# Moving an attention kernel's input loads into one software DMA queue, with the last rows grouped per head pair

## Chip, cores, metric

The kernel runs on one core of one Trainium2 chip. The metric is device time in microseconds (us), the median of several executions. Single-core executions of one kernel mostly agree within about 1% here. A span in a profile is that of one profiled execution, about 2 us shorter than its timed value.

## The reference, cut to what matters

```python
# q, k, v: (8 batches, 8 heads, 576 rows, 64) float32; w_phi: (64, 128)
def phi(x):
    proj = einsum('bhsd,df->bhsf', x, w_phi)
    proj = proj - max(abs(proj), -1)
    return concatenate([exp(proj), exp(-proj)], -1)
# linear attention: num = phi(q) @ (phi(k)^T v), den = phi(q) @ sum(phi(k)); x = num/den
# then, per batch on (576, 512):
X = rfft(x, axis=1)[:64 modes];  Y = X (complex) times w_r + i w_i per mode  # 64 x 512 x 512, twice
u = x + irfft(Y);  out = u + relu(u @ w_ch)                                   # w_ch: 512 x 512
```

The two weight tensors are 134 MB of float32, q, k and v together 28 MB. Everything else is small.

## The kernel before

The attention stage handles 16 units: 4 head pairs `g` times 4 batch pairs `bp`. Loads are issued by two engines. POOL issues loads on the software queue, here with a cast from float32 to bfloat16 on the way; SP (the sync engine) issues loads on the hardware queue, here without a cast. Rows 512 to 575 of each (batch, head), the "tails", come separately:

```python
def load(t, rest, src, g, bp, eng):
    for i in range(2):
        hs = src[2 * bp + i, 2 * g:2 * g + 2]
        sp.dma_start(rest[64 * i:64 * i + 64],                       # tail: 128 runs of 256 B, hardware queue
                     hs[:, 512:576, :].rearrange("h p d -> p h d"))
        eng.dma_start(                                               # main: 128 partitions x 2 x 1 KB
            t[:, 8 * i:8 * i + 8, :].rearrange("p (h c) d -> p h (c d)", h=2),
            hs[:, 0:512, :].rearrange("h (p c) d -> p h (c d)", c=4))
# k, q: main by POOL with cast, tail as float32 and cast by VectorE (cast_k, cast_q)
# v:    main and tail by SP, float32
```

Weights come as 64 tiles of 1 MB (bfloat16, 2 MB read) by POOL, in eight rotating buffers (five early tiles sit elsewhere). Each is used by one `mix`; a mix frees its buffer and the next tile is issued. After the attention loop, PE runs the remaining 22 mixes and 36 `channels` steps (x @ w_ch), which need `wchb`, the bfloat16 copy of w_ch:

```python
    wchb = const.tile([128, 4, 512], BF16, name="wchb")
...
        if n == 6:                                   # in the attention loop
            pool.dma_start(wchb, moe_w_ch.rearrange("(dc p) e -> p dc e", p=128))
...
pm_cm.__exit__(...); pin_cm.__exit__(...)            # attention memory ends
pb = pb_cm.__enter__()
while mixq:
    mix(...); next_w(1)                              # next_w issues one weight tile
    for _ in range(2):
        if todo: channels(*todo.pop(0))
```

Each engine works off a fixed list. In the built program PE's order at this point is: mix 42, mix 43, four channels, mix 44, mix 45, four channels, and so on (counted from zero).

The softmax here doesn't subtract the row's maximum and nothing guards it: scores larger than these inputs give would overflow.

## Time and profile before

| | before |
|---|---|
| time, median of 3 | 481.94 us (481.29 to 482.75) |
| span of the profiled execution | 481.0 us |
| mix 43 starts | 325.0 us |
| first channels step | 326.1 us |
| last mix (tile 63) starts | 432.9 us |
| output stage starts | 438.7 us |

From the page of the kernel before: span, DMA busy in 40 slices (9 is 90% or more), the two load queues, the chain that ended last, and some DMA issues (size, median us from issue to landing). PE multiplies matrices, DVE is VectorE, ACT is ScalarE.

```profile
span 481.0 us, 8083 instructions
...
DMA  8999999999999999999999999999999999990676
...
q0 software_dynamic: 84496, 76.03, 97.2%
q1 hardware_dynamic: 26784, 23.14, 18.4%
...
DMA 9%; PE 9%; ACT 0%; DVE 0%; issue 0%; POOL 0%; ACTq 0%; POOLq 0%
...
wt<-in_moe_w_i_dram POOLq DMA_DIRECT2D x30, 1024.0 KB, 27.1
...
vn<-in_v_dram SPq DMA_DIRECT2D x32, 256.0 KB, 8.0
...
kb<-in_k_dram POOLq DMA_DIRECT2D x32, 128.0 KB, 20.9
```

The packets of the software queue took 97% of the 16 engines' span. A weight tile waits 27 us to land, while v on the hardware queue takes 8 us.

From the table by windows of the same kernel: length and busy us per engine, then PE's granted clock, DMA share and GB/s written. A share above 1 means packets overlap on an engine.

```profile
12.00:330.00 318.00, 220.34 (x2472) 153.66 (x2469) 236.10 (x429) 201.74 (x345) 83.13 (x105) 0.82 1.25 210
330.00:430.00 100.00, 67.02 (x478) 30.74 (x477) 20.64 (x43) 27.98 (x49) 10.49 (x12) 0.95 1.23 212
```

The DMA share stays at the same level through both stages, so I take DMA to pace the kernel up to 430 us; the chain that ended last agrees, with 43.9 us of DMA for the last weight tile.

From PE's timeline (start, duration, engine, line, operation, count, and in brackets the idle time before it and what ended it):

```profile
319.99 0.69 PE L37 MATMUL one<-wt,XT_69 128*32 128x512 bf16 x8 [2.78 <-DMA wt<-in_moe_w_r_dram]
...
325.04 1.09 PE L37 MATMUL one<-wt,XT_69 128*32 128x512 bf16 x8 [4.03 <-DMA wt<-in_moe_w_i_dram]
326.06 1.89 PE L469 MATMUL one<-wchb,xT 128*128 128x512 bf16 x4
...
432.87 1.09 PE L37 MATMUL one<-wt,XT_70 128*32 128x512 bf16 x8 [5.06 <-DMA wt<-in_moe_w_i_dram]
...
438.70 0.58 PE L607 MATMUL pt<-xs,ident_b 128*128 128x512 bf16 x1 [0.72 <-ACT zst L37]
```

These are mixes 42 and 43, the first channels step (wchb long there), the last mix and the start of the output stage. Between 325 and 433 us the mixes wait now and then for their tile, but those waits are only about 15 us out of the 112 us from 326.1 to 438.7 us: PE has little slack.

### The profile page before, as it was taken

How to read it: one execution, taken by the hardware profiler on the slowest of the kernel's cores; microseconds unless marked ns; L12 is line 12 of the kernel's file. 1: busy time of each engine (PE TensorE's matmuls, PEld its weight loads, DVE VectorE, ACT ScalarE, POOL GpSimd, SP SyncE). 2: the span in 40 equal slices, each digit the busy share in tenths (PEclk: the TensorE clock that was granted, in tenths of full speed). 3: DMA queues.
4: the chain of work that ended last, by engine and by line, in shares of the span. 5: the costliest groups of instructions: out<-in, count | busy, mean ns of one | idle time of the engine just before them, and what ended most of it. 6: DMA issues, size and time to landing. Idle time of an engine off the chain costs nothing. (4 is left out here: it accounts for less than half of the span.)

```text
span 481.0 us, 8083 instructions
## 1 busy us (share of the span) xinstructions
PE 329.9 (69%) x3133; PEld 202.0 (42%) x3133; DVE 288.8 (60%) x524; ACT 256.4 (53%) x435; POOL 103.9 (22%) x139
## 2 busy tenths in 40 slices
PE   2563786778877876876597546827667676738994
PEld 1351554555555544654365334613233332312441
DVE  5777579778679779778869747622222121100874
ACT  3771867867867965865675737401223232301763
POOL 8332222123312331322033121221111110000000
PEclk9956879777889988878977959788899999965998
DMA  8999999999999999999999999999999999990676
GB/s 137 212 213 210 210 209 210 214 213 191 216 210 211 213 215 207 214 216 205 215 218 203 220 204 207 207 207 208 207 207 218 214 214 214 215 178 22 241 296 251
DMA packets 111318, 99.68 MB, mean 207 GB/s; under 512 B 16944, under 2 KB 109744, under 8 KB 110256
## 3 DMA queue, kind: packets, MB, share of 16 engines
q0 software_dynamic: 84496, 76.03, 97.2%
q1 hardware_dynamic: 26784, 23.14, 18.4%
q8 instruction: 24, 0.39, 0.3%
q14 instruction: 14, 0.11, 0.1%
HBM read 163.64 MB, written 9.44 MB: 360 GB/s over the span
## 5 line engine op out<-in xcount | busy, mean ns | idle before, releaser
L37 ACT ACTIVATE AB<-two 128x1024 bf16<-128x1024 f32 x64 | 62.0, 1021 | 44.3 <-DVE mk L37 43.9
L37 ACT ACTIVATE AQ<-two 128x1024 bf16<-128x1024 f32 x64 | 62.6, 1042 | 17.4 <-PE two L37 17.3
L471 ACT CAST xw<-one 128x512 bf16<-128x512 f32 x36 | 21.1, 585 | 68.8 <-PE one L469 57.6
L466 DVE COPY xT<-one 128x512 bf16<-128x512 bf16 x36 | 15.3, 424 | 63.9 <-PE one L464 63.9
L37 POOL DMA_DIRECT2D wt<-in_moe_w_r_dram x29 | 25.6, 882 | 111.5 <-PE one L37 66.3
L469 PE MATMUL one<-wchb,xT 128*128 128x512 bf16 x144 | 39.0, 395 | 14.0 <-DVE xT L466 14.0
L37 PE MATMUL one<-va,AB 128*128 128x65 bf16 x512 | 31.8, 227 | 20.6 <-DVE va L37 20.6
L37 DVE TENSOR_TENSOR va<-vn,ee 128x1152 bf16<-128x1152 f32 x32 | 41.9, 1352 | 0.0
L37 DVE TENSOR_REDUCE mk<-two 128x8 f32<-128x1024 f32 x32 | 39.0, 1218 | 4.0 <-PE two L37 4.0
L37 PE MATMUL one<-kvz,AQ 128*128 128x65 bf16 x512 | 30.2, 205 | 15.5 <-ACT kvz L37 10.7
L37 DVE TENSOR_REDUCE mq<-two 128x8 f32<-128x1024 f32 x32 | 37.6, 1215 | 1.1 <-PE two L37 1.1
L37 PEld LDWEIGHTS <-AB 128*128 128x128 bf16 x512 | 26.8, 120 | 26.7 <-DVE va L37 13.1
L37 POOL DMA_DIRECT2D wt<-in_moe_w_i_dram x30 | 26.4, 880 | 49.8 <-PE one L37 19.3
L37 PEld LDWEIGHTS <-AQ 128*128 128x128 bf16 x512 | 25.8, 106 | 26.3 <-issue 23.0
L37 POOL DMA_DIRECT2D qb<-in_q_dram x32 | 22.9, 719 | 57.3 <-PE one L37 16.3
L37 POOL DMA_DIRECT2D kb<-in_k_dram x32 | 22.9, 717 | 52.7 <-DMA wt<-in_moe_w_i_dram 17.5
L37 PE MATMUL one<-ident_b,kb 128*128 128x128 bf16 x144 | 15.3, 254 | 25.0 <-DMA kb<-in_k_dram 16.1
L620 DVE TENSOR_TENSOR of<-pt,rl 128x512 f32<-128x512 f32 x32 | 21.7, 690 | 15.1 <-ACT rl L618 14.8
L37 PE MATMUL one<-wt,XT_70 128*32 128x512 bf16 x256 | 20.6, 418 | 14.6 <-DMA wt<-in_moe_w_i_dram 11.9
L37 DVE TENSOR_TENSOR nd<-one,nd 128x390 f32<-128x390 f32 x48 | 27.1, 565 | 5.7 <-PE two L37 0.5
L618 ACT ACTIVATE rl<-pt 128x512 f32<-128x512 f32 x36 | 21.4, 597 | 15.3 <-PE pt L609 12.4
L37 PE MATMUL one<-CF,xs 128*128 128x256 bf16 x160 | 26.7, 327 | 2.3 <-DVE xs L37 2.3
(125 smaller groups left out, 620.5 us busy)
## 6 DMA issues: line engine op xcount, KB each, us to landing
wt<-in_moe_w_i_dram POOLq DMA_DIRECT2D x30, 1024.0 KB, 27.1
wt<-in_moe_w_r_dram POOLq DMA_DIRECT2D x29, 1024.0 KB, 26.5
vn<-in_v_dram SPq DMA_DIRECT2D x32, 256.0 KB, 8.0
out_dram<-of SPq DMA_DIRECT2D x8, 1024.0 KB, 3.9
kb<-in_k_dram POOLq DMA_DIRECT2D x32, 128.0 KB, 20.9
qb<-in_q_dram POOLq DMA_DIRECT2D x32, 128.0 KB, 17.1
kf<-in_k_dram SPq DMA_DIRECT2D x32, 32.0 KB, 6.1
vn<-in_v_dram SPq DMA_DIRECT2D x32, 32.0 KB, 6.8
```

Of the source, the lines that this page charges most:

```text
L37: ins = f(*args, **kwargs)
L466: nc.vector.tensor_copy(xT, pt)
L469: nc.tensor.matmul(pf, lhsT=xT[:, g, :], rhs=wchb[:, g, :], start=(g == 0), stop=(g == 3))
L471: nc.scalar.copy(xw[:, bp, n, :], pf)
L618: nc.scalar.activation(rl, ps[1], ACT.Relu)
L620: nc.vector.tensor_tensor(out=o, in0=ps[0], in1=rl, op=ALU.add)
```

## The change

The intent is to drop the hardware queue's many small loads and VectorE's casts: everything goes through the software queue, v too but without a cast, and the tails of a head pair are fetched once for all batches (4 loads per tensor and head pair, in place of 2 per unit and tensor). The grouped tails need more memory, so wchb no longer fits beside the attention stage and moves behind it.

```diff
-    def load(t, rest, src, g, bp, eng):
+    def load(t, src, g, bp, eng):                       # main part only, as before
...
+    def load_rests(name, src, g, eng):
+        t = pin.tile([128, NP, 2, D_], F32 if name == "v" else BF16, name=name + "r")
+        for i in range(2):
+            for h in range(2):
+                eng.dma_start(
+                    t[64 * i:64 * i + 64, :, h, :],
+                    src[i::2, 2 * g + h, 512:576, :].rearrange("b p d -> p b d"))
+        rests[name, g] = t
...                                                      # cast_k, cast_q gone; va multiply regrouped
-                unit(n + 3).load_v()                     # by SP
+                unit(n + 3).load_v(pool)
+        if n >= 0 and n % 4 == 0 and n // 4 + 1 < NG:    # behind load_k
+            load_rests("k", k, n // 4 + 1, pool)
+        if n >= 0 and n % 4 == 1 and n // 4 + 1 < NG:    # behind load_v
+            load_rests("q", q, n // 4 + 1, pool)
+            load_rests("v", v, n // 4 + 1, pool)
...
-    wchb = const.tile([128, 4, 512], BF16, name="wchb")
-        if n == 6:
-            pool.dma_start(wchb, ...)
+    wchb = pb.tile([128, 4, DMODEL], BF16, name="wchb", bufs=1)      # behind the attention loop
+    nc.gpsimd.dma_start(wchb, ...)
```

The v of the first two units and the v tails of the first head pair still come by SP.

More of the change, by code (lines that the diff above doesn't have):

```diff
@@ L87 @@
     pm = pm_cm.__enter__()
-    def load(t, rest, src, g, bp, eng):
+    def load(t, src, g, bp, eng):
         for i in range(2):
-            hs = src[2 * bp + i, 2 * g:2 * g + 2]
-            sp.dma_start(
-                rest[64 * i:64 * i + 64],
-                hs[:, 512:576, :].rearrange("h p d -> p h d"),
-            )
             eng.dma_start(
                 t[:, 8 * i:8 * i + 8, :].rearrange("p (h c) d -> p h (c d)", h=2),
-                hs[:, 0:512, :].rearrange("h (p c) d -> p h (c d)", c=4),
-            )
+                src[2 * bp + i, 2 * g:2 * g + 2, 0:512, :].rearrange(
+                    "h (p c) d -> p h (c d)", c=4),
+            )
+    rests = {}
+    def load_rests(name, src, g, eng):
[6 more added lines that the diff above has]
+        rests[name, g] = t
     class Unit:
@@ L107, in load_k, with load_v, turn @@
         def load_k(self):
-            self.kb = pin.tile([128, 18, D_], BF16, name="kb")
-            self.kf = pin.tile([128, 2, D_], F32, name="kf")
-            load(self.kb, self.kf, k, self.g, self.bp, pool)
-        def cast_k(self):
-            dve.tensor_copy(self.kb[:, 16:18, :], self.kf)
-        def load_q(self):
-            self.qb = pin.tile([128, 18, D_], BF16, name="qb")
-            self.qf = pin.tile([128, 2, D_], F32, name="qf")
-            load(self.qb, self.qf, q, self.g, self.bp, pool)
-        def cast_q(self):
-            dve.tensor_copy(self.qb[:, 16:18, :], self.qf)
-        def load_v(self):
-            self.vn = pin.tile([128, 18, D_], F32, name="vn")
-            load(self.vn, self.vn[:, 16:18, :], v, self.g, self.bp, sp)
-        def turn(self, src, name):
+            self.kb = pin.tile([128, 16, D_], BF16, name="kb")
+            load(self.kb, k, self.g, self.bp, pool)
+        def load_q(self):
+            self.qb = pin.tile([128, 16, D_], BF16, name="qb")
+            load(self.qb, q, self.g, self.bp, pool)
+        def load_v(self, eng):
+            self.vn = pin.tile([128, 16, D_], F32, name="vn")
+            load(self.vn, v, self.g, self.bp, eng)
+        def turn(self, src, rest, name):
             dst = pm.tile([128, 9, 128], BF16, name=name, tag="xT", bufs=3)
             flat = src.rearrange("p n d -> p (n d)")
+            rest = rest[:, self.bp].rearrange("p h d -> p (h d)")
             for lo, hi in ((0, 4), (4, 9)):
@@ L133, in turn @@
                 for j in range(lo, hi):
-                    pe.transpose(ptr[:, j - lo, :], flat[:, j * 128:(j + 1) * 128], ident_b)
+                    x = flat[:, j * 128:(j + 1) * 128] if j < 8 else rest
+                    pe.transpose(ptr[:, j - lo, :], x, ident_b)
                 act.copy(dst[:, lo:hi, :], ptr)
@@ L138, in turn_k @@
         def turn_k(self):
-            self.kT = self.turn(self.kb, "kT")
+            self.kT = self.turn(self.kb, rests["k", self.g], "kT")
             self.mk = pm.tile([128, 2, 18], F32, name="mk")
         def turn_q(self):
-            self.qT = self.turn(self.qb, "qT")
+            self.qT = self.turn(self.qb, rests["q", self.g], "qT")
             self.mq = pm.tile([128, 18], F32, name="mq")
@@ L191, in weigh_v2 @@
             dve.tensor_copy(self.va[:, :, :, 64], ee)
-            for ab in range(2):
+            for n0, n1, x in ((0, 16, self.vn), (16, 18, rests["v", self.g][:, self.bp])):
+                shape = [128, 2, n1 - n0, 64]
                 dve.tensor_tensor(
-                    out=self.va[:, ab, :, 0:64], in0=self.vn,
-                    in1=ee[:, ab, :].unsqueeze(2).to_broadcast([128, 18, 64]), op=ALU.mult,
+                    out=self.va[:, :, n0:n1, 0:64], in0=x.unsqueeze(1).to_broadcast(shape),
+                    in1=ee[:, :, n0:n1].unsqueeze(3).to_broadcast(shape), op=ALU.mult,
                 )
@@ L320 @@
     units[0].load_k()
-    units[0].load_v()
+    load_rests("k", k, 0, pool)
+    units[0].load_v(sp)
+    load_rests("v", v, 0, sp)
     units[0].load_q()
+    load_rests("q", q, 0, pool)
     w2blk = const.tile([128, 256], BF16, name="w2blk")
@@ L495 @@
     units[1].load_k()
-    units[1].load_v()
+    units[1].load_v(sp)
     next_w(1)
@@ L499 @@
     next_w(1)
-    units[0].cast_k()
     units[0].turn_k()
@@ L523 @@
                 mixq += [(P.g, mg) for mg in range(2 * NO)]
-        if K:
-            K.cast_q()
         if Q:
             Q.num(0)
-        if R:
-            R.cast_k()
         if K:
@@ L569 @@
         some(X - 4)
-        if n == 6:
-            pool.dma_start(wchb, moe_w_ch.rearrange("(dc p) e -> p dc e", p=128))
     for e in (pe, dve, act, pool, sp):
@@ L578 @@
     pb = pb_cm.__enter__()
+    wchb = pb.tile([128, 4, DMODEL], BF16, name="wchb", bufs=1)
+    nc.gpsimd.dma_start(wchb, moe_w_ch.rearrange("(dc p) e -> p dc e", p=128))
     xw = pb.tile([128, NP, 9, DMODEL], BF16, name="xw", bufs=1)
```

## The prediction

> **What bounds the kernel now.** The table by windows gives a DMA share of 1.23 to 1.26 from 12 to 410 us (packets overlap). Most loads stand in the software queue: a 1 MB weight tile takes 26.5 us from issue to landing (DMA issues), the last ones 43.9 us. Fitting packet counts to elapsed time, I estimate per engine and packet: weights (1 KB) 79.8 ns, q/k (512 B) 43, v (1 KB, hardware queue) 53, tails (256 B) 26. So a weight tile costs 5.1 us, and 64 of them 327 us. The chain of waits ends with 43.9 us of DMA for the last weight tile (to 432.8 us), then 48 us of final mix and output.
>
> **What the change does.**
> 1. Tails: 12,288 packets before and after, but 48 issues instead of 96, now mostly on the software queue, q and k cast to 128 B. Cost before 768 x 26 ns = 20 us per engine. The Trainium skill (DMA: Bandwidth & Descriptors, Specifications) says that under 512 B the engine does read-modify-write; the trace shows only 256 B at 26 ns. I expect 15 to 28 ns: -8 to +2 us.
> 2. v: 512 packets per engine, 53 ns to 43-50 ns: -1 to -5 us.
> 3. DVE loses 32 casts of 0.22 us; the va multiply keeps its element count. Little is critical.
> 4. POOL issues some 106 more small loads at 0.71 us (75 us). The program lets only eight software-queue loads be outstanding (each waits for the eighth before it), so runs of 12 to 22 small loads leave little queued: I expect short DMA gaps where the tails go, 2 to 8 us in all.
>    Sum of 1 to 4: the stream to weight tile 49 gains about 2 us (-6 to +8).
> 5. wchb moves. It was loaded at 156 us, needed at 326 us. Now it takes over memory of the attention stage and stands in the POOL order behind weight tile 49. The queue being first in first out (43.9 us for eight tiles agrees), wchb lands just after tile 49, which the timeline shows arriving at 355.4 us. In PE's program order its first user (channels) follows mix 43 (done at 326.1 us), and PE cannot pass it. So PE stands still until about 354 us, then has nearly all of the second stage to do: 326.1 to 438.7 us before, about 15 us of it waits for weight tiles, so 97.5 us of PE chain. It was just hidden under DMA (10.1 us of PE chain, 10.2 us of DMA per two tiles), so PE can't catch up.
>
> **Sum.** 355.4 - 2 + 97.5 + 42.3 (output stage, 438.7 to 481) = 493 us, plus 1 us for time over span, plus about 2 us [...]: **496 us, range 488 to 507**. Chances: faster 0.02, within 2% 0.23, slower 0.75.
>
> **What would show it.** PE (channels) waits some 28 us once for wchb; POOL issues the last weight tile after 400 us; the chain that ended last is PE/DVE/ACT from about 354 us on rather than DMA. kb/qb land sooner, v later (8 us to about 15-20 us).
>
> **What would make it wrong.** Tails or v much cheaper in the software queue, or attention freed by 10 us or more (then within 2%); wchb landing earlier than tile 49; a late v stalling DVE, or DMA gaps over 10 us (then above 500).

## The result, and the profile after

The changed kernel took 500.52 us (median of 4, 500.29 to 503.86) against 481.62 us (median of 4). The ratio is 1.0408, 95% interval 1.0358 to 1.0458. Ratios here and below are the mean time of one kernel's fast runs over that of the other's of the same rounds, so not quite the ratio of the medians quoted.

From the page of the changed kernel, the same lines:

```profile
span 498.5 us, 7899 instructions
...
DMA  9999999999999999999999999999999999961576
...
q0 software_dynamic: 95824, 85.21, 103.3%
q1 hardware_dynamic: 6432, 12.91, 7.5%
...
PE 8%; ACT 1%; DVE 1%; DMA 1%; issue 0%; ACTq 0%
...
wt<-in_moe_w_i_dram POOLq DMA_DIRECT2D x30, 1024.0 KB, 19.2
...
vn<-in_v_dram POOLq DMA_DIRECT2D x28, 256.0 KB, 14.1
kb<-in_k_dram POOLq DMA_DIRECT2D x32, 128.0 KB, 14.2
```

The chain that ended last was half DMA and half PE (9% of the span each); now it is nearly all PE (8%, DMA 1%). A weight tile now lands after 19 us, which fits with less standing ahead of it in the queue. From the table by windows:

```profile
12.00:330.00 318.00, 207.72 (x2434) 146.49 (x2449) 231.46 (x396) 201.65 (x343) 129.25 (x173) 0.83 1.20 200
330.00:430.00 100.00, 51.47 (x361) 23.55 (x367) 16.32 (x34) 20.72 (x36) 12.28 (x14) 0.80 1.19 202
```

The DMA share fell from 1.25 to 1.20 and from 1.23 to 1.19. The first figure looks small; over 318 us it is about 13 us of lost DMA time. From PE's timeline:

```profile
326.31 1.10 PE L37 MATMUL one<-wt,XT 128*32 128x512 bf16 x8 [2.75 <-DMA wt<-in_moe_w_r_dram]
...
331.33 1.09 PE L37 MATMUL one<-wt,XT 128*32 128x512 bf16 x8 [3.38 <-DMA wt<-in_moe_w_i_dram]
364.40 0.58 PE L474 MATMUL one<-wchb,xT 128*128 128x512 bf16 x1 [31.98 <-DMA wchb<-in_moe_w_ch_dram]
...
458.06 0.38 PE L612 MATMUL pt<-xs,ident_b 128*128 128x512 bf16 x1 [0.72 <-ACT zst L37]
```

Mix 43 comes 6.3 us later than before (331.33 against 325.04). Then PE stands still for 32.0 us until wchb lands. Weight tiles had been landing about 5.07 us apart (the mixes that waited for tiles 43 and 49 started at 325.04 and 355.44 us before). Six tiles and wchb, half a tile, make 6.5 x 5.07 = 33.0 us; from 331.33 to 364.40 is 33.1 us. So wchb came exactly in its turn. From 364.40 to 458.06 us PE works off what it had hidden under DMA before.

To see where the DMA time went, I added up the packets' times in each microsecond, divided by 16 engines, and summed what is missing to 1.24, the undisturbed level; the sum over 12 to 330 us, divided by 1.24, is called the shortfall below. It is 3.7 us before and 19.0 us after. (Where the microseconds are cut moves these sums by up to 0.6 us, so smaller differences of the shortfall mean nothing.) The largest holes after are at 62 to 64, 92 to 94, 164 to 166 and 243 to 248 us. POOL's timeline shows the second of them:

```profile
78.50 1.30 POOL L37 DMA_DIRECT2D qr<-in_q_dram  x2
84.21 0.62 POOL L37 DMA_DIRECT2D qr<-in_q_dram  x1 [4.41 <-DMA wt<-in_moe_w_i_dram]
89.25 0.61 POOL L37 DMA_DIRECT2D qr<-in_q_dram  x1 [4.43 <-DMA xs<-in_moe_w_r_dram]
89.89 2.09 POOL L37 DMA_DIRECT2D vr<-in_v_dram  x3
92.18 0.62 POOL L37 DMA_DIRECT2D vr<-in_v_dram  x1 [0.20 <-DMA qr<-in_q_dram]
92.79 1.45 POOL L37 DMA_DIRECT2D qb<-in_q_dram  x2
94.21 0.93 POOL L37 DMA_DIRECT2D xs<-in_moe_w_i_dram  x1
```

The q tails (`qr`) wait for weight tiles to land although they need nothing from them. The built program explains it. Every load on the software queue takes one of eight semaphores in turn and waits until the load that used it last has landed. POOL's order in the built changed kernel, numbered in its own list, with those waits (DMASW is the semaphore):

```
57 vn<-in_v_dram 128x2x256 [waits DMASW1_49,DVE_49]
58 vn<-in_v_dram 128x2x256 [waits DMASW2_49]
59 qr<-in_q_dram 64x4x64 [waits DMASW3_49]
60 qr<-in_q_dram 64x4x64 [waits DMASW4_49]
61 qr<-in_q_dram 64x4x64 [waits DMASW5_49]
62 qr<-in_q_dram 64x4x64 [waits DMASW6_49]
63 vr<-in_v_dram 64x4x64 [waits DMASW7_49]
...
69 xs<-in_moe_w_i_dram 128x8x512 [waits DMASW5_49]     (a weight tile)
```

So the tails hold up POOL until the weight tiles ahead have landed. When the last of them has (89.2 us), only small loads are outstanding, and POOL needs some 5 us to issue seven more small loads before the next weight tile follows at 94.2 us. DMA runs dry meanwhile. All in all POOL waited 22.8 + 17.7 us at q tails for weight tiles. From its list of waits (who waited for what, us in total, times, longest):

```profile
POOL qr L37 <- DMA wt<-in_moe_w_i_dram: 22.8, 5, 5.0
POOL qr L37 <- DMA wt<-in_moe_w_r_dram: 17.7, 4, 5.0
```

POOL waits for weight tiles before the change too (17.5 us at kb loads, for example). What is new is how much small work follows: counted in the built programs, behind the start, the longest stretch of small loads between two weight tiles grows from 8 to 20.

The packets of v got cheaper, and the others hardly changed (packet records of the two traces; sizes are those written):

| packet | before | after |
|---|---|---|
| v main | 1 KB, 58.9 ns, hardware queue | 4 KB, 174.6 ns with the v tails (median 159), software queue: 44 ns per KB |
| k, q tails | 256 B, 30.5 ns | 128 B, 32.3 ns |
| v tails | 256 B, 30.5 ns | the same 4 KB packets, 16 runs in one |
| k, q main | 512 B, 60.0 ns | 512 B, 62.1 ns |
| weights | 1 KB, 97.8 ns | 1 KB, 99.3 ns |

Counts times these times, over 16 engines and 1.24, make 5.5 us saved on v, 3.5 us on v's tails (those of the first head pair included, 21 ns each on the hardware queue), and 0.7 us lost on k's and q's tails: an estimated 8.3 us saved. Mix 43 should then shift by +15.3 (shortfall) - 8.3 (packets) - 2.5 (wchb no longer ahead of it) = +4.5 us; measured is +6.3. The sum is rough: the longer packets of the weights and of k's and q's main loads are left out, and counted the same way they would add an estimated 5 us (44 tiles by 1.5 ns, 16384 packets by 2.1 ns), more than the 1.8 us missing. So the balance holds only to a few us.

### The profile page after: what moved, and what is told of

The parts are those of the page before. It is cut to its first block, busy times and chain, and to the rows that moved or that the text cites. A ratio compares the mean times of both kernels' runs of the same rounds, so it can differ in the third digit from the quotient of the medians.

```text
span 498.5 us, 7899 instructions
## 1 busy us (share of the span) xinstructions
PE 314.1 (63%) x3104; PEld 194.6 (39%) x3133; DVE 284.5 (57%) x492; ACT 256.5 (51%) x435; POOL 152.2 (31%) x211
## 5 line engine op out<-in xcount | busy, mean ns | idle before, releaser
L471 DVE COPY xT<-one 128x512 bf16<-128x512 bf16 x36 | 15.3, 425 | 96.7 <-PE one L469 96.7
L37 DVE TENSOR_TENSOR nd<-one,e 128x390 f32<-128x390 f32 x48 | 26.8, 559 | 48.2 <-PE one L37 48.2
L37 DVE TENSOR_REDUCE mk<-two 128x8 f32<-128x1024 f32 x32 | 39.0, 1220 | 19.2 <-PE two L37 18.8
L37 PE MATMUL one<-kvz,AQ 128*128 128x65 bf16 x512 | 29.1, 203 | 25.9 <-ACT kvz L37 20.3
L37 PE MATMUL one<-wt,XT 128*32 128x512 bf16 x472 | 39.1, 440 | 9.6 <-DMA wt<-in_moe_w_i_dram 3.4
L37 PE MATMUL one<-va,AB 128*128 128x65 bf16 x512 | 26.2, 212 | 27.0 <-DVE va L37 27.0
L37 DVE TENSOR_TENSOR va<-vn,ee 128x2048 bf16<-128x2048 f32 x16 | 36.6, 2289 | 0.0
L474 PEld LDWEIGHTS <-xT 128*128 128x128 bf16 x144 | 11.4, 100 | 63.8 <-issue 34.2
L37 PEld LDWEIGHTS <-AB 128*128 128x128 bf16 x512 | 22.2, 110 | 32.3 <-DVE va L37 28.4
L37 POOL DMA_DIRECT2D vn<-in_v_dram x28 | 20.7, 749 | 32.4 <-DMA wt<-in_moe_w_i_dram 6.6
L37 PEld LDWEIGHTS <-XT 128*32 128x32 bf16 x512 | 20.5, 171 | 23.1 <-issue 13.5
## 6 DMA issues: line engine op xcount, KB each, us to landing
vn<-in_v_dram POOLq DMA_DIRECT2D x28, 256.0 KB, 14.1
kb<-in_k_dram POOLq DMA_DIRECT2D x32, 128.0 KB, 14.2
```

Source lines behind the costliest of these rows:

```text
L37: ins = f(*args, **kwargs)
L471: nc.vector.tensor_copy(xT, pt)
L474: nc.tensor.matmul(pf, lhsT=xT[:, g, :], rhs=wchb[:, g, :], start=(g == 0), stop=(g == 3))
```

## The experiments

Ten runs. All gave correct results. `hw` in a label means that wchb comes early enough through the hardware queue. "Last mix" is the start of the mix of tile 63. Every interval excludes 1. Against a line of 2%, only changed and before_tiny count as slower; before_wchb_late, after_wchb_hw and after_hw_spread may lie on either side of it, and the others are within it.

| run | ratio to before (95%) | median us | shortfall us | last mix us |
|---|---|---|---|---|
| before | 1 | 481.6 to 483.4 | 3.7 | 432.9 |
| changed | 1.0408 (1.0358 to 1.0458) | 500.52 | 19.0 | not DMA-paced |
| before_wchb_late | 1.0184 (1.0148 to 1.0220) | 491.52 | 3.5 | not DMA-paced |
| after_wchb_hw | 1.0224 (1.0185 to 1.0263) | 493.72 | 18.2 | 442.2 |
| after_hw_v_sp | 1.0159 (1.0122 to 1.0196) | 490.66 | 15.4 | 442.6 |
| after_hw_vr_sp | 1.0153 (1.0125 to 1.0182) | 488.94 | 14.6 | 439.1 |
| after_hw_spread | 1.0171 (1.0138 to 1.0204) | 491.35 | 18.8 | 441.8 |
| after_hw_spread_w | 1.0069 (1.0035 to 1.0104) | 486.66 | 14.4 | 438.9 |
| before_tiny | 1.0340 (1.0316 to 1.0365) | 498.68 | 14.7 | 448.9 |
| before_v_sw | 0.9915 (0.9873 to 0.9958) | 479.22 | 7.8 | 432.3 |
| before_v_sw_5 | 0.9902 (0.9886 to 0.9918) | 478.43 | 7.0 | 431.5 |
| before_v_sw_w | 0.9952 (0.9923 to 0.9981) | 480.42 | 7.5 | 432.7 |

### 1. wchb alone

The kernel before, with only wchb moved to where the change has it.

```diff
-    wchb = const.tile([128, 4, 512], BF16, name="wchb")
-        if n == 6:
-            pool.dma_start(wchb, ...)
     pb = pb_cm.__enter__()
+    wchb = pb.tile([128, 4, DMODEL], BF16, name="wchb", bufs=1)
+    nc.gpsimd.dma_start(wchb, ...)
```

> The kernel before with one part of the change alone: the wchb load goes behind weight tile 49 in memory of the ended attention stage; all other loads untouched. Theory (wchb late stops PE): no new DMA gaps before 330 us, PE waits 26 to 31 us once for wchb, which lands at about 355 us, then 93.6 us of PE chain and 40.5 us of output as in the changed kernel: 488 to 493 us. Rival (the loss comes from the loads alone, PE has slack to catch up): 481 to 484 us.

Measured: ratio 1.0184, about 9 us. PE's timeline of this run:

```profile
322.11 1.09 PE L37 MATMUL one<-wt,XT 128*32 128x512 bf16 x8 [3.44 <-DMA wt<-in_moe_w_i_dram]
355.16 1.87 PE L468 MATMUL one<-wchb,xT 128*128 128x512 bf16 x4 [31.95 <-DMA wchb<-in_moe_w_ch_dram]
...
448.95 0.38 PE L606 MATMUL pt<-xs,ident_b 128*128 128x512 bf16 x1 [0.72 <-ACT zst L37]
```

The shortfall is that of the kernel before, and mix 43 is even 2.9 us earlier, as wchb's half tile no longer stands ahead of it. The PE stop alone costs 9 us; the rival, that PE has slack to catch up, falls. The PE chain from wchb to the output took 448.95 - 355.16 = 93.8 us.

### 2. The loads alone

The changed kernel, with wchb fetched through the hardware queue, past the software queue. The attention memory it lies in must be free first, as in the change, so wchb is complete at about 337 us, its first part from 327 us, and not at 171 us as in the kernel before.

```diff
     wchb = pb.tile([128, 4, DMODEL], BF16, name="wchb", bufs=1)
-    nc.gpsimd.dma_start(wchb, moe_w_ch.rearrange("(dc p) e -> p dc e", p=128))
+    for dc in range(4):
+        wchf = pb.tile([128, DMODEL], F32, name="rl")
+        nc.sync.dma_start(wchf, moe_w_ch[128 * dc:128 * dc + 128, :])
+        nc.vector.tensor_copy(wchb[:, dc, :], wchf)
```

> The changed kernel, but wchb comes through the sync queue in float32 in four pieces and is cast on VectorE, so it does not stand behind eight weight tiles. Theory (two separate costs, each about half): wchb ready at about 333 to 340 us instead of 364, PE waits under 10 us for it, the end is set by the last weight tile again, about 439 us, 6 us later than before because of DMA gaps: 486 to 491 us. Rival A (all of the loss was wchb): 480 to 484 us. Rival B (the PE stop was harmless, the loads are all of it): 498 to 502 us.

Measured: ratio 1.0224, about 11 us over before; the median, 493.72, is 3 us above the range I gave, the profiled span 490.0 us.

```profile
333.38 1.09 PE L37 MATMUL one<-wt,XT 128*32 128x512 bf16 x8 [4.53 <-DMA wt<-in_moe_w_i_dram]
334.40 0.61 PE L474 MATMUL one<-wchb,xT 128*128 128x512 bf16 x1
...
442.20 1.10 PE L37 MATMUL one<-wt,XT 128*32 128x512 bf16 x8 [4.59 <-DMA wt<-in_moe_w_i_dram]
```

PE no longer stops for wchb, and the end is DMA-paced again, 9.3 us later than before. (Mix 43 is 2 us later than in the changed kernel; the float32 wchb, 512 packets of 2 KB, now comes partly ahead of it, which may be why.) The two halves, 1.84% and 2.24%, add up to the whole, 4.08%. They add because wchb's turn comes behind tile 49, and the loads delay tile 49: wchb came at 355.16 us in experiment 1 and at 364.40 us in the changed kernel.

### 3. Which loads: v or the tails

v's main loads alone into the software queue, in the kernel before:

```diff
-            load(self.vn, self.vn[:, 16:18, :], v, self.g, self.bp, sp)
+            load(self.vn, self.vn[:, 16:18, :], v, self.g, self.bp, pool)
```

> The kernel before with one part alone: v's large loads and last rows stay as they are in shape, but the large ones go to the software queue without a cast (tails stay on the sync queue per unit). Theory (v's packets become 4 KB packets of 159 ns, cheaper than 4 x 59 ns; the gaps come from runs of tail loads, not from v): DMA gaps before 330 us under 7 us, last weight tile 5 to 9 us earlier, 473 to 479 us. Rival (v in the POOL order is what empties the queue): gaps of 8 us or more, 483 to 490 us.

And the reverse, v's main loads back to SP in the kernel of experiment 2, so that only the tails differ from the kernel before (and wchb's path):

```diff
-                unit(n + 3).load_v(pool)
+                unit(n + 3).load_v(sp)
```

> The same as the run with wchb through the sync queue, but v's large loads go back to the sync queue, so only the tails (48 loads per run of the kernel, 44 in the software queue) and their grouping are left of the load changes. Theory (runs of small tail loads fill the eight outstanding places and empty the queue; v's move itself saves time): gaps of 10 us or more remain, and the time is 4 to 10 us over the run with v in the software queue: 491 to 498 us. Rival (v makes the gaps): gaps under 6 us, 482 to 487 us.

v alone makes the kernel slightly faster, not slower (0.9915; repeated in five rounds below, 0.9902). The tails alone make it slower by 1.6%, with a shortfall of 15.4 us. So the tails make most of the holes. (The time, 490.66 us, is just under the 491 to 498 I gave.) Beside the tails v's move gains nothing: with v on SP the ratio is 1.0159, with v in the software queue (experiment 2) 1.0224, though the two profiled executions have the same span, 490.0 us. Whether it costs something there stays open. My sizes for v were off, though: I expected the last tile 5 to 9 us earlier and got 0.6. Its packets saved 6.7 us by the same sum as above (v main 24.3 us before; 17.6 us in the software queue), but the shortfall grew by 4 us, most of it near 113 us. POOL's timeline of this run shows why:

```profile
107.40 1.44 POOL L37 DMA_DIRECT2D qb<-in_q_dram  x2 [0.50 <-DVE nd L37]
112.84 0.89 POOL L37 DMA_DIRECT2D wt<-in_moe_w_i_dram  x1 [4.00 <-PE one L37]
```

Weight tile 13 (from zero) is the first that needs a freed buffer, after eight in the rotating buffers and five elsewhere, and it waits for PE. The places for weights are full before the first head pair is done, so DMA time saved before that has nothing to be spent on.

### 4. Is it the number of loads or their bytes

The kernel before, plus 36 loads of 2 KB that nobody reads, in the runs of 4 and 8 where the change has its tails.

```diff
+        if n >= 0 and n % 4 < 2 and n // 4 + 1 < NG:
+            for _ in range(4 + 4 * (n % 4)):
+                tiny = pin.tile([64, 16], BF16, name="tiny", bufs=8)
+                pool.dma_start(tiny, q[0, 0, 0:64, 0:16])
```

> The kernel before plus 36 loads of 2 KB each (64 rows of 32 B) that nobody reads, in runs of 4, 8, 4, 8, 4, 8 in the software queue where the changed kernel puts its tail loads. They add loads but almost no bytes. Theory (what costs is that a run of small loads takes the eight outstanding places, so POOL waits for weight tiles to land and the queue runs empty): DMA gaps before 330 us grow from 3.7 us to 10 us or more, the last weight tile lands 5 to 10 us later, 487 to 492 us. Rival (the tail's 128 B packets or their bytes cost the time, not their number): gaps under 6 us, 481 to 485 us.

Measured: ratio 1.0340, 16 us, with almost no bytes; at 498.68 us well above the 487 to 492 I gave. POOL's timeline shows the same picture as the tails did:

```profile
80.12 0.53 POOL L37 DMA_DIRECT2D tiny<-in_q_dram  x1 [6.65 <-DMA wt<-in_moe_w_r_dram]
81.16 1.11 POOL L37 DMA_DIRECT2D tiny<-in_q_dram  x2 [0.51 <-DMA qb<-in_q_dram]
87.25 0.52 POOL L37 DMA_DIRECT2D tiny<-in_q_dram  x1 [4.98 <-DMA wt<-in_moe_w_i_dram]
94.56 0.52 POOL L37 DMA_DIRECT2D tiny<-in_q_dram  x1 [6.80 <-DMA xs<-in_moe_w_r_dram]
```

The rival (bytes, or the 128 B packets) falls. The shortfall explains 11 us of the 16; the 2304 packets of 32 B took 24.9 ns each, about 3 us by the same sum; the last 2 us I cannot place.

Taking away instead of adding, v's 12 later tail loads alone go to SP, in the kernel of experiment 2:

```diff
-            load_rests("v", v, n // 4 + 1, pool)
+            load_rests("v", v, n // 4 + 1, sp)
```

> The run with wchb through the sync queue, with v's tail loads alone (12 of the 36 later ones) moved to the sync queue; grouping, bytes and number of loads unchanged. Theory (each small load in the software queue costs one of eight outstanding places, so the loss goes with their number there): DMA gaps before 330 us fall from 18 us to 10 to 14 us, last weight tile 2 to 5 us earlier than 442.2, 487 to 491 us. Rival (the loss comes from grouping the tails for four batches, or from k's and q's 128 B packets): 492 to 495 us, gaps unchanged.

Twelve small loads fewer: shortfall 18.2 to 14.6 us, last mix 3.1 us earlier, ratio 1.0153 against 1.0224 (the two intervals, of different rounds, just fail to meet). Grouping and bytes are unchanged, so the gain does not come from them.

### 5. Does it help to spread them

The 36 later tail loads, three to an iteration, one behind each of the k, v and q loads, in the kernel of experiment 2 (cut):

```diff
+    todo_r = [(nm, s, g, j) for g in range(1, NG)
+              for nm, s in (("k", k), ("q", q), ("v", v)) for j in range(4)]
...
+            one_rest()                # behind load_q, and likewise behind load_k and load_v
-            load_rests("k", ...) / load_rests("q", ...) / load_rests("v", ...)
```

> The run with wchb through the sync queue, with the same 48 tail loads, but the 36 later ones put three to an iteration (one behind each of the k, v and q loads) instead of in runs of 4 and 8. Theory (runs make the gaps): gaps before 330 us fall from 18 us to 5 to 10 us, the last weight tile lands at 432 to 437 us instead of 442, 480 to 486 us. Rival (number of small loads, wherever they stand): gaps and time unchanged, 490 to 495 us.

This theory of mine, that runs of tail loads are what hurts, fell: shortfall 18.8 against 18.2 us, last mix 441.8 against 442.2 us. The ratio is 1.0171, so the time may be a little better, but the holes only moved (112 to 115 us and 118 to 119 us are now the largest). Each small load takes one of eight places, whether it is a tail or not: with the k, v and q loads counted, the longest stretch between two weight tiles is 18 small loads in the built program, against 20 before the spreading.

In the same kernel one weight tile moved from iteration 2 to iteration 3. The built program shows that this cuts the stretch of 18 small loads near 115 us into two of 9, but not a second stretch of 18 later on, which I had overlooked:

```diff
-        if n < 3:
-            next_w((2, 2, 2, 2)[n + 1])
+        if n < 4:
+            next_w((2, 2, 2, 1, 1)[n + 1])
```

> As the spread run, and one weight tile of iteration 2 moved to iteration 3, which cuts the longest run of small loads from 18 to 10. Theory: the gap near 115 us goes, gaps under 6 us in all, 2 to 4 us faster than the spread run: 476 to 483 us, the first version of the changed loads that is faster than the kernel before. Rival: no difference from the spread run.

It gains some 5 us (ratio 1.0069, shortfall 14.4 us). It does not get below the kernel before, although I had expected 476 to 483 us and under 6 us of holes: the hole near 115 us shrank but stayed, and another lies at 162 to 165 us. A large load between small ones does help, where its buffer is free.

The runs together suggest what counts. Add up, over all stretches between two weight tiles behind the start, the small loads beyond the eighth (counted in the built programs): 0 before, 6 with v alone, 14 in before_tiny, 16 in after_hw_spread_w and after_hw_v_sp, 18 in after_hw_vr_sp, 24 in after_hw_spread, 30 in the changed kernel. The shortfalls, 3.7, 7.8, 14.7, 14.4, 15.4, 14.6, 18.8 and 19.0 us, come in nearly that order. Only before_v_sw_w below stands out (2 and 7.5 us): there a tile waits for its buffer. This was read off afterwards; no run was made to test it.

The same move with v alone in the software queue:

> The kernel before with v's large loads in the software queue, and one weight tile of iteration 2 moved to iteration 3, so that the run of 12 small loads where the queue stood empty near 113 us is cut. Theory: gaps before 330 us fall from 7.8 us to about 4 us, the last weight tile lands 4 to 6 us before the kernel before's, 475 to 479 us. Rival (v in the software queue saves nothing and the gap has another cause): 478 to 483 us.

No further gain over v alone (0.9952 against 0.9915; shortfall 7.5 against 7.8 us). There the tile must wait for its buffer, as in experiment 3, and moving it does not change that. The expected fall to 4 us was wrong, and so was the time (480.42 us, not 475 to 479).

### 6. The version that beats both

The kernel of experiment 3 with v's main loads alone in the software queue, in five rounds.

> The kernel with v's large loads alone in the software queue, again, in five rounds, since its gain was under 1%: 477 to 481 us, ratio 0.988 to 0.997. If the first result was chance, the ratio is within 0.997 to 1.003.

Ratio 0.9902, interval 0.9886 to 0.9918. So one part of the change, v's main loads in the software queue, is worth 1% alone, clear of the noise though under the 2% line. The profiled executions show a gain of only 1.0 and 1.7 us in the span, the medians of the timed runs about 4 us; both profiled executions were the slowest of their runs. Where the difference lies is open.

## Why the prediction was right

The predicted 496 us (488 to 507) holds the measured 500.5 us, and slower by over 2% was called.

- **wchb stops PE (step 5): right.** PE waited 32.0 us where 28 were predicted. wchb landed in its turn behind tile 49. The Trainium skill (DMA: Bandwidth & Descriptors, SWDGE vs HWDGE vs iDMA, on two DMAs through the same engine) says that within one queue of a DMA engine descriptors start in order. This trace agrees: wchb took 37.4 us from issue to landing, which is 4.5 us for the rest of tile 43 and, by the spacing of 5.07 us, an estimated 30.4 us for tiles 44 to 49 and 2.5 us for itself. The chain that ended last lost its DMA part (9% to 1%), and the last weight tile was issued at 420.9 us ("after 400").
- **PE cannot catch up: right.** The PE chain from wchb on took 93.7 us (97.5 predicted), the output stage 40.4 us (42.3). Both were shorter than predicted, and the 2 us added to the sum for the clock were not needed: the clock granted to PE was 0.97 over the chain and 0.94 in the output stage, against 0.91 (326.1 to 438.7 us) and 0.90 before. The sum reads 364.4 + 93.7 + 40.4 = 498.5 us, the span. Experiment 1 shows this part alone: 9 us.
- **The load stream (sum of 1 to 4) "gains about 2 us (-6 to +8)": wrong in size and sign.** It lost about 9 us: wchb landed at 364.4 us, in the place where tile 49 had arrived at 355.4 (6.3 us of it are seen at mix 43, and 2.5 the removal of wchb hid there). The mis-sized term is step 4: "short DMA gaps where the tails go, 2 to 8 us in all". They were 15 us (19.0 against 3.7). The prediction had itself listed "DMA gaps over 10 us (then above 500)" under what would make it wrong, and that came true: 15 us and 500.5 us. The mechanism was the named one, eight outstanding loads, but not only with tails in a run: the spread tails made the same shortfall. The count in this step was off as well: POOL issued 72 more loads, not 106 (28 of v, 44 tails), and was busy 48 us longer (103.9 to 152.2 us), not 75.
- **v's packets (step 2): right in sign, larger than expected.** 44 ns per KB at the mean against 59; the software queue put four 1 KB runs into one 4 KB packet. Whether the packet's size or the queue is the reason was not tested.
- **Tails (step 1): no saving for k and q.** The prediction cited the same page (Specifications) on less than 512 B. Its 26 ns for 256 B was a fit to elapsed time; the packet records say 30.5. The 128 B packets took 32.3 ns where 256 B took 30.5: half the bytes written, from the same 256 B read and in the other queue, saved nothing.
- **kb and qb land sooner, v later: right.** kb 20.9 to 14.2 us, qb 17.1 to 9.4 us, v 8.0 to 14.1 us (15 to 20 predicted).
- **The closeness of the total is partly luck.** wchb came 11 us later than the 353.4 us of the sum. The chain (3.8 us), the output (1.9) and the clock allowance (2) made up most of that, so 496 us came within 5 us of 500.5.

What stays open: whether the eight places or POOL's own issue time (some 0.6 to 0.7 us for a small load) is the tighter limit within a hole. In the hole at 92 us POOL had first waited for places and was then busy issuing. The number of places is set by the program's build, and I found no way to raise it; halving the tail loads by merging two heads in one load did not build (more dimensions than a load may have).

## What to carry to other kernels

When a queue allows a fixed number of loads outstanding, its depth in bytes depends on the mean load size, so every small load put into the queue of the big ones takes a place worth a big load; count loads, not only bytes, and count how many stand between two big ones. When memory forces a load to a later place, ask what stands ahead of it in a first-in-first-out queue, and what an in-order engine cannot do until it lands. Work hidden under DMA with no slack (here about 10.1 us of PE against as much of DMA for two tiles) must not be started late.

## What the Trainium skill lacked or had wrong

- DMA: Bandwidth & Descriptors, Issuing engine by pattern, says that the hardware queues (sync/scalar) are generally faster. Here that held for v's main loads from issue to landing (8.0 us before, 14.1 us in the software queue of the changed kernel), but not for their time on the DMA engines: 4 KB software packets at 170.5 ns mean (159 median) in before_v_sw against 4 x 58.9 ns on the hardware queue, and the kernel with v alone moved was 1% faster (0.9902).
- The same page, Rules for kernel authors, tells to merge many small transfers, as under 64 KB one pays mostly overhead. It has no number for what small loads cost the large ones beside them when a program lets eight be outstanding: 36 loads of 2 KB cost 16 us here (0.45 us each), and 12 loads of 64 KB moved off the queue gave back 3.4 us.
- Trainium Kernel Development and Optimization, Key Constraints, says that issuing DMAs from several engines only saves the sequencer's issue time. It gives no size for what that can be worth. Here, moving 12 tail loads from POOL's queue to SP's changed the time by 0.7% (1.0224 to 1.0153). Issue time may be part of it (0.6 to 0.7 us of POOL each), and so may the places freed, since each queue has its own eight semaphores in this built program. No run parts the two, so nothing here contradicts the page.
- DMA: Bandwidth & Descriptors, Specifications, gives a threshold of 512 B. What it lacks is packet times below it beside a full stream of weights: here 32.3 ns for 128 B written with a cast, 30.5 ns for 256 B without, and 60 ns for 512 B with a cast.
